# Residual rows one tile ahead, and a sum that takes its third chunk last, in a four-layer kernel

## The chip, the cores and the metric

The kernel runs on one core of a Trainium2 chip. The metric is the time of one execution on the device in microseconds (us), the median over several runs. A run has engines that work in order, each through its own queue: PE (matrix products; PEld is its weight load), DVE (vector work), ACT (activations and copies), POOL (elementwise work), and SP, which here only issues transfers (DMAs). They wait for each other through semaphores.

## The reference

Four layers on one sequence of 2048 rows by 640 columns, in float32: attention, Fourier mixing, attention, Fourier mixing, each added to its input.

```python
x = A_x
x = x + _A_ref(_layernorm(x), A_wqkv, A_wo)      # 32 heads of 20, window of 256
x = x + _B_ref(_layernorm(x), dft matrices)
x = x + _A_ref(_layernorm(x), A_wqkv, A_wo)
x = x + _B_ref(_layernorm(x), dft matrices)

def _A_ref(x, wqkv, wo):
    q, k, v = split(x @ wqkv)
    scores = where(0 <= i - j < 256, q @ k.T * 20 ** -0.5, -1e9)
    return merge(softmax(scores) @ v) @ wo
def _B_ref(x, re, im, dre, dim):
    return re @ (x @ dre.T) - im @ (x @ dim.T)
```

The change lies in the two attention layers: in `x @ wqkv` for the values (the first layer alone) and in the `x + ... @ wo` at the end (both).

## The kernel before

**Products in three parts.** Factors of the projections are split into a high and a low part, and a product of two split factors is three matmuls: high·high, high·low, low·high (`product3`, lines 253 to 260, called by `all3`). The 640 columns over which a projection sums are five chunks of 128, so a sum is 15 matmuls into one PSUM bank.

**The start of an attention layer** (`before_heads`). Rows are handled in 16 row tiles of 128. For each, `prep` requests rows, takes the mean and variance on DVE (`prep_stats`), the root on POOL (line 311), normalises on DVE (line 316), transposes on PE (line 363) and splits the transposed tile into high and low parts. The value weights come in five chunks (`value_weights`): each is loaded, copied to its high part by ACT (line 380), and its low part is the rest of a subtraction (line 383). In the first layer POOL makes the low parts of chunks 0, 1 and 2, and DVE those of 3 and 4. Chunks 0 to 2 lie in the tile `qp`, 3 and 4 in two tiles `pt`. `value(t)` then makes the two half-width sums (320 columns each, line 471) of row tile t. Row tile 0 is the first work of that kind on PE.

**The heads** (`heads`). 128 steps (8 groups of four heads by 16 row tiles) go through the engines in an order written at build time. PE makes scores twice, rows by keys (line 677) for the row maximum, which DVE takes with the mask (line 682), and keys by rows (line 705) for the exponential on ACT (line 715), which POOL masks (lines 721 and 725); line 740 multiplies by the values. The negated row maximum travels through a small transpose (line 690), a copy to the tile `mt` on ACT (line 693), and two DMAs into a row of `qp` (line 695), from where the products of line 705 take it up. Row sums travel through the DMA `sm<-ou` (line 759) to a reciprocal on DVE (line 762).

**What fills the gaps between steps** (`fill`, `more`). First comes the projection of the remaining queries and keys (`project`). When that is done, `partials` follows, in the last third of a layer's heads: for each of 16 row tiles it multiplies three of the five chunks of the heads' results by `wo` (line 275, 36 half-height matmuls), and DVE adds the sum to the row tile's residual rows. For row tiles 0 to 4 ACT first copies the sum out of PSUM (line 1046) and DVE adds it a few slots later (line 1047); from row tile 5 on DVE adds straight from PSUM (line 1050). In the profile the residual rows are the tile `big`, in `y_part(t)`, and they come by the DMAs of line 1016 (`load_y`). Row tiles 7 and 15 need three requests (112, 15 and 1 rows), since rows are stored shifted by one there.

**When residual rows are requested.** `prepare(4)`, called when the projection's last product has been written, posts the requests of the first `AHEAD_X` row tiles, row tile t after 4t slots (a step has two slots). At the head of row tile t `partials` requests row tile `t + AHEAD_X`:

```python
        elif n == 4:
            self.take_big(2, F32)
            for t in range(AHEAD_X):
                self.post(4 * t, lambda t=t: self.load_y([t]))
...
        for t in range(NB):
            sb, i = t // 4, t % 4
            self.load_y([t + AHEAD_X])
```

**The queue of transfers.** All DMAs are issued by SP, in the order of the program. They take eight semaphores in turn, and a DMA waits until the one issued eight places before it on the same semaphore has landed. So a request can start long after the place in PE's order at which the program wrote it. An instruction that reads a loaded tile waits for that DMA's semaphore, and whatever stands behind it in its engine's queue waits too.

Of the kernel before, what the change touches and what calls it, by code (L numbers as in the profile page):

```python
# [19 lines left out]
KC = D // P  # L20
# [10 lines left out]
LEAD = 10  # L31
AHEAD = 8
EARLY = 3
AHEAD_X = 2
ROWS_AT = 96
LAST_DUE = (-8, -3, 0, 4)
FIRST = 7
# [36 lines left out]
class Net:  # L74
# [336 lines left out]
    def before_heads(self, xsrc):  # L411
        nc, a = self.nc, self.a
        self.proj = self.project()
        first = self.first
        vst = [t.rearrange("p (q t c) -> p q t c", t=2, c=96) for t in self.pt[:2]]
        for v in self.pt[:2]:
            (nc.vector if first else nc.gpsimd).memset(v, 1.0)
        for t in range(6):
            self.prep_load(xsrc, t)
            if first and 2 < t < 5:  # L420
                self.load_chunk(t - 3)
        if first:
            mask = self.raw()[:, :384]
            nc.sync.dma_start(mask, a["mask"])
        self.prep_stats(0)
        self.prep_stats(1)
        self.prep_norm(0)
        state = [0, 6]
        here = self.ou + self.rr
        wv = self.wv  # L430

        def check():
            here.append(here.pop(0))
            self.check_step(here[0][:, :8 * WIDE])

        def prep():
            r = state[0]
            if state[1] < r + 5:
                self.prep_load(xsrc, state[1])
                state[1] += 1  # L440
            self.prep_stats(r + 2)
            self.prep_norm(r + 1)
            if r == 10 or r == 11:
                self.prep_norm(r + 2)
            if r == 11:
                self.prep_stats(14)
                self.prep_stats(15)
                self.prep_norm(14)
            if r == 12:
                self.prep_norm(15)  # L450
            self.prep_turn(r)
            state[0] += 1

        def pieces(sb):
            for c in range(2):
                if sb == 0:
                    prep()
                self.piece(c, sb, "q")
                if c or sb > 1 or not first:
                    check()  # L460
                if sb and state[0] < 4 * sb + 8:
                    prep()

        def value(t):
            v, xt = vst[t // 2 % 2], self.xnt(t // 4)
            rs = slice((t % 4) * P, (t % 4 + 1) * P)
            ps = []
            for hf in range(2):
                p = self.bank("v", 320)
                cs = slice(hf * 320, (hf + 1) * 320)  # L470
                self.all3(p, [((xt[:, 0, k, rs], xt[:, 1, k, rs]), (wv[k][0][:, cs], wv[k][1][:, cs]))
                              for k in range(KC)])
                ps.append(p)
            prep()
            for hf in range(2):
                dst = v[:, 4 * hf:4 * hf + 4, t % 2, 0:84].rearrange("p q (h c) -> p q h c", c=21)[:, :, :, 1:21]
                src = ps[hf].rearrange("p (q h c) -> p q h c", q=4, h=4)
                if hf == 0:
                    nc.scalar.activation(dst, src, AF.Copy)
                else:  # L480
                    nc.vector.tensor_copy(dst, src)  # L481
            if t % 2:
                nc.sync.dma_start(self.vd[:, :, t - 1:t + 1, :].rearrange("q p t c -> p q (t c)"),
                                  v.rearrange("p q t c -> p q (t c)"))
            if 3 < t < 14 or t < 4 and not first:
                check()
            elif t > 13:
                for _ in range(t - 13):
                    self.check_step()

        def values(sb):
            for i in range(4):
                value(4 * sb + i)

        def packed(sb):
            for f in self.pack(0, sb):
                f()

        self.split_w(4)
        prep()  # L500
        self.split_w(6)
        prep()
        self.split_w(3 * KC)
        for t in range(4):
            if t in (1, 2):
                self.cut_chunk(t - 1)
            value(t)
        if first:
            nc.gpsimd.tensor_copy(self.mask, mask)
        while state[1] < NB:  # L510
            self.prep_load(xsrc, state[1])
            state[1] += 1
        pieces(0)
        pieces(1)
        self.take_qk("kp", 0)
        self.ones_rows(0)
        packed(0)
        packed(1)
        values(1)
        pieces(2)  # L520
        self.load_chunk(2)
        packed(2)
        values(2)
        pieces(3)
        self.cut_chunk(2)
        self.load_chunk(3)
        packed(3)
        values(3)
        while self.stages:
            self.check_step()  # L530
        self.pt += [self.slot_tile(f"pt{i}", 3 * 512, F32) for i in (2, 3)]
        for name in ("kp", "qp"):
            self.take_qk(name, 1)
        self.ones_rows(1)
# [426 lines left out]
    def prepare(self, n):  # L961
# [28 lines left out]
# [4 lines that stand above are left out]
# [24 lines left out]
    def partials(self, xsrc):  # L1018
# [5 lines left out]
# [3 lines that stand above are left out]
            y = self.y_part(t)  # L1027
# [695 lines left out]
```

## Time and profile before

| | |
|---|---|
| median of 3 runs | 1360.11 us (1353.72 to 1364.23) |
| profiled execution, its own time | 1360.81 us |
| its span (first to last instruction) | 1359.0 us |
| mean granted PE clock | 0.989 |
| PE busy | 1292.3 us (95%) |
| DVE busy | 969.7 us (71%) |
| ACT, POOL busy | 765.1 us (56%), 733.7 us (54%) |
| DMA queue of SP | 259 MB, 63.5% of the 16 DMA engines' time |
| requests of line 1016, first attention layer | 20, from 424.5 to 508.7 us |
| requests of line 1016, second attention layer | 20, from 1094.5 to 1180.2 us |

A timeline row gives start and duration in us, engine, line, operation, the tile written and those read, and how many instructions stand together; the bracket is how long the engine sat idle before it and what released it. SPq is SP's queue of DMA issues: its duration is that of the issue, not of the transfer. In a row of stretches the numbers after each engine are its busy time and, in brackets, its instructions; then come the granted PE clock, the share of the DMA engines' time, and GB/s. Busy shares are means over stages with different limits, so a wait is judged in its own stage.

### The profile page before, as it was taken

Reading aid. Unit: us, or ns where it says so; the run is one execution under the profiler, and the core shown is the slowest. Engines: PE = TensorE matmul, PEld = TensorE weight load, DVE = VectorE, ACT = ScalarE, POOL = GpSimd, SP = SyncE. Lnnn points to the kernel's source line nnn. Section 1 sums busy time; section 2 is a strip of 40 time slices with the busy share of each in tenths; the row PEclk is TensorE's granted clock in tenths of the full one; section 3 lists DMA queues with packets and bytes.
Section 4 is the critical chain, followed back from the end, with each engine's and each line's share of the span. In section 5 each row is a group of like instructions: output and inputs, shape, how many; then the busy total and the mean of one; then the engine's idle time right before and its main releaser. Section 6 shows DMA issues by size and latency. Waiting matters only on the chain. (4 is left out here: it accounts for less than half of the span.)

```text
span 1359.0 us, 37437 instructions
## 1 busy us (share of the span) xinstructions
PE 1292.3 (95%) x13350; PEld 992.9 (73%) x13350; DVE 969.7 (71%) x3117; ACT 765.1 (56%) x1661; POOL 733.7 (54%) x1508
## 2 busy tenths in 40 slices
PE   6999999999998999999999999999999989989996
PEld 6899777777776777743689997777777767777344
DVE  7723788888887865765866247888888868658674
ACT  3322378777776665446323225777777755744472
POOL 4221677777877773310334237787777866723044
PEclk9999999999999999989999999999999989999999
DMA  5675566777677875436536755776777688671565
GB/s 198 215 226 167 188 200 199 206 195 214 201 223 219 209 235 154 135 94 210 194 117 201 227 164 185 198 207 196 220 201 225 202 217 209 197 217 47 178 209 198
DMA packets 174297, 261.49 MB, mean 192 GB/s; under 512 B 36306, under 2 KB 85586, under 8 KB 174100
## 3 DMA queue, kind: packets, MB, share of 16 engines
q1 hardware_dynamic: 174100, 259.00, 63.5%
q8 instruction: 108, 1.77, 0.6%
q14 instruction: 89, 0.73, 0.2%
HBM read 175.42 MB, written 82.31 MB: 190 GB/s over the span
## 5 line engine op out<-in xcount | busy, mean ns | idle before, releaser
L682 DVE CUSTOM_DVE_ANT_0 banks<-banks,mask 128x384 f32<-128x384 f32 (+2 forms) x1024 | 527.4, 557 | 118.7 <-PE banks L677 99.7
L715 ACT ACTIVATE pt<-banks 128x768 f32<-128x768 f32 (+2 forms) x512 | 394.4, 772 | 141.3 <-PE banks L705 72.4
L721 POOL TENSOR_SCALAR_AFFINE_SELECT pt<-pt 128x256 f32<-128x256 f32 x512 | 223.2, 436 | 181.8 <-ACT pt L715 158.7
L275 PE MATMUL banks<-big,wc 64*128 64x512 f32 x1920 | 272.5, 394 | 0.4 <-DVE pt L481 0.4
L705 PE MATMUL banks<-qp,kp 61*128 61x384 f32 (+2 forms) x1024 | 209.5, 379 | 19.6 <-DVE mc L682 14.0
L677 PE MATMUL banks<-kp,qp 60*128 60x384 f32 (+2 forms) x1024 | 209.7, 353 | 6.2 <-DVE mc L682 5.8
L740 PE MATMUL banks<-pt,vq 128*32 128x128 f32 x5760 | 211.9, 278 | 0.9 <-ACT pt L715 0.8
L275 PEld LDWEIGHTS banks<-big,wc 64*128 64x128 f32 x1920 | 187.7, 185 | 21.8 <-ACT x L590 1.5
L725 POOL TENSOR_SCALAR_AFFINE_SELECT pt<-pt 128x256 f32<-128x256 f32 x448 | 187.0, 417 | 0.0
L740 PEld LDWEIGHTS banks<-pt,vq 128*32 128x32 f32 x5760 | 142.6, 110 | 48.9 <-issue 35.2
L705 PEld LDWEIGHTS banks<-qp,kp 61*128 61x128 f32 x1024 | 107.9, 184 | 82.6 <-DVE mc L682 57.4
L677 PEld LDWEIGHTS banks<-kp,qp 60*128 60x128 f32 x1024 | 124.3, 186 | 33.6 <-DVE mc L682 22.1
L682 DVE DVE_READ_ACCUMULATOR2_ANT mc<- 128x1 f32 x1024 | 145.1, 142 | 0.0
L749 ACT ACTIVATE ou<-banks 128x128 f32<-128x128 f32 (+2 forms) x288 | 73.4, 267 | 61.9 <-PE banks L740 50.9
L257 PE MATMUL banks<-qp,big 128*128 128x320 f32 x576 | 98.4, 316 | 1.0 <-POOL qp L383 1.0
L229 POOL TENSOR_TENSOR c<-x,c 128x256 fp32r<-128x256 f32 x128 | 94.4, 745 | 0.0
L257 PEld LDWEIGHTS banks<-qp,big 128*128 128x128 f32 x576 | 88.3, 191 | 1.6 <-POOL qp L383 1.4
L257 PE MATMUL banks<-qp,kp 128*128 128x320 f32 x384 | 82.2, 347 | 6.8 <-ACT big L1132 4.4
L275 PE MATMUL banks<-big,big 64*128 64x320 f32 x912 | 80.2, 312 | 0.2 <-ACT mt L693 0.2
L257 PEld LDWEIGHTS banks<-qp,kp 128*128 128x128 f32 x384 | 61.0, 188 | 20.2 <-ACT big L1132 6.5
L1508 POOL TENSOR_TENSOR rr<-rr 128x171 f32<-128x171 f32 (+3 forms) x76 | 48.2, 644 | 49.0 <-DMA rr<-hr 18.5
L275 PEld LDWEIGHTS banks<-big,big 64*128 64x128 f32 x912 | 73.1, 189 | 0.4 <-ACT mt L693 0.4
(172 smaller groups left out, 1790.4 us busy)
## 6 DMA issues: line engine op xcount, KB each, us to landing
qk_d<-c SPq DMA_DIRECT2D x80, 512.0 KB
kp<-qk_d SPq DMA_DIRECT2D x384, 80.0 KB
qp<-qk_d SPq DMA_DIRECT2D x384, 80.0 KB
o_d<-ou SPq DMA_DIRECT2D x64, 256.0 KB
v_d<-pt SPq DMA_DIRECT2D x16, 768.0 KB
vq<-v_d SPq DMA_DIRECT2D x64, 192.0 KB
kp<-ki SPq DMA_DIRECT2D x44, 228.0 KB
big<-x SPq DMA_DIRECT2D x26, 320.0 KB
```

The costliest lines, as they stand in the source:

```text
L229: eng.tensor_tensor(out=lo[..., c], in0=src[..., c], in1=hi[..., c].bitcast(F32), op=OP.subtract)
L257: self.nc.tensor.matmul(p, x, y, start=n == 0, stop=n == last)
L275: self.nc.tensor.matmul(ps[a], x[r], y[r], start=half + i == 0, stop=half == 1 and i == n - 1, skip_group_check=True)
L677: nc.tensor.matmul(p, qp[quad % 2][b:b + 60, z, qb * P:(qb + 1) * P], kp[quad % 2][b:b + 60, z, k0 * P:(qb + 1) * P], start=True, stop=True)
L682: nc.vector.tensor_tensor_reduce(out=p, in0=p, in1=self.mask[:, 384 - n * P:], scale=1.0, scalar=NEG, op0=OP.add, op1=OP.max, accum_out=mc ...
L705: nc.tensor.matmul(self.banks[:, banks[e], :n * P], kp[quad % 2][b:b + 61, z, kb * P:(kb + 1) * P], qp[quad % 2][b:b + 61, z, kb * P:(kb + ...
L715: nc.scalar.activation(pt[quad, kb][:, 2 * z:2 * z + 2, :n * P], self.banks[:, b0:b1 + 1, :n * P], AF.Exp, scale=SCALE)
L721: nc.gpsimd.affine_select(out=t[:, :, 0:P], in_=t[:, :, 0:P], pattern=[[0, 2], [1, P]], compare_op=OP.is_ge, fill=0.0, base=0, channel_mul ...
L725: nc.gpsimd.affine_select(out=t[:, :, 256:384], in_=t[:, :, 256:384], pattern=[[0, 2], [-1, P]], compare_op=OP.is_gt, fill=0.0, base=0, ch ...
L740: nc.tensor.matmul(self.banks[32 * h:32 * h + 32, bank, :P], vq[:, 96 * (kb % 4) + 21 * h:96 * (kb % 4) + 21 * h + 32], t[:, h, (qb - kb) ...
L749: nc.scalar.activation(ou[:, dst], self.banks[:, bank, src], AF.Copy)
L1508: eng.tensor_tensor(out=t[:, lo:hi], in0=t[:, lo:hi], in1=base.broadcast_to([P, hi - lo, w]), op=op)
```

## The change

Two edits. The constant `AHEAD_X` goes from 2 to 1: `prepare(4)` posts one request and not two, and each `partials` tile requests the row tile after it and not the one after that. It holds in both attention layers. And in the first attention layer, row tile 0 of the values sums its chunks in the order 0, 1, 3, 4, 2; all other sums keep theirs.

```diff
-AHEAD_X = 2
+AHEAD_X = 1
...
                 self.all3(p, [((xt[:, 0, k, rs], xt[:, 1, k, rs]), (wv[k][0][:, cs], wv[k][1][:, cs]))
-                              for k in range(KC)])
+                              for k in ((0, 1, 3, 4, 2) if first and t == 0 else range(KC))])
                 ps.append(p)
```

On PE, at the start of the program, the two sums of row tile 0 stood so (`qp` holds the weights of chunks 0 to 2, three matmuls each, the two `pt` those of 3 and 4; line 363 is the transposes of row tiles 0 and 1 ahead and of row tile 2 behind):

```order
L363 MATMUL banks<-ident,big_109 128x128 x10
L257 MATMUL banks<-qp_113,big_164 128x320 x9
L257 MATMUL banks<-pt_115,big_164 128x320 x3
L257 MATMUL banks<-pt_116,big_164 128x320 x3
L257 MATMUL banks<-qp_113,big_164 128x320 x9
L257 MATMUL banks<-pt_115,big_164 128x320 x3
L257 MATMUL banks<-pt_116,big_164 128x320 x3
L363 MATMUL banks<-ident,big_109 128x128 x5
```

and stand so now:

```order
L363 MATMUL banks<-ident,big_109 128x128 x10
L257 MATMUL banks<-qp_113,big_164 128x320 x6
L257 MATMUL banks<-pt_115,big_164 128x320 x3
L257 MATMUL banks<-pt_116,big_164 128x320 x3
L257 MATMUL banks<-qp_113,big_164 128x320 x9
L257 MATMUL banks<-pt_115,big_164 128x320 x3
L257 MATMUL banks<-pt_116,big_164 128x320 x3
L257 MATMUL banks<-qp_113,big_164 128x320 x3
L363 MATMUL banks<-ident,big_109 128x128 x5
```

The three matmuls of chunk 2 moved behind those of chunks 3 and 4 in each half. Row 5 now holds chunk 2 of the first half and chunks 0 and 1 of the second.

On SP in the first attention layer, at the place where row tile 1 was requested (the DMAs around it are the row sums and reciprocals of lines 759 to 765, the reload of finished heads of lines 904 and 910, and, a little behind, the row maxima `mt` of line 695):

```order
 L760 DMA o_d<-ou_105 128x512
 L765 DMA r_d<-rc 128x16
-L1016 DMA big_6148<-x 128x640
 L904 DMA x<-o_d 128x1x512
 L910 DMA rr_106<-r_d 128x1x512
```

One request is gone there. Row tile 1 is now requested where row tile 2 was, seven issues earlier, and every later row tile where the one after it was.

On SP further on, around the request of row tile 7, which is the three of 112, 15 and 1 rows (`kp` and `qp` from `qk_d` are the next heads' factors, `vq` their values, `big_6191` is the tile of row tiles 8 to 15):

```order
 L640 DMA kp_1248<-qk_d 20x2x512 x3
+L1016 DMA big_6148<-x 128x640
+L640 DMA qp_1249<-qk_d 20x2x512 x3
+L667 DMA vq_100<-v_d 128x384
+L640 DMA qp_1249<-qk_d 20x2x512 x3
 L1016 DMA big_6148<-x 112x640
 L1016 DMA big_6148<-x 15x640
 L1016 DMA big_6148<-x 1x640
-L640 DMA qp_1249<-qk_d 20x2x512 x3
-L667 DMA vq_100<-v_d 128x384
-L640 DMA qp_1249<-qk_d 20x2x512 x3
-L1016 DMA big_6191<-x 128x640
```

The request of row tile 6 (one of 128 rows) now stands where row tile 7's three stood, and row tile 7's three where row tile 8's was, seven DMAs of other kinds later. The second attention layer has the same order. DVE, ACT and POOL keep their orders in both layers.

## The prediction

> **What bounds the kernel now.** I read the page first, then the timeline of each engine in the places that the change touches, then PE's waits.
>
> ```profile
> span 1359.0 us, 37437 instructions
> PE 1292.3 (95%) x13350; PEld 992.9 (73%) x13350; DVE 969.7 (71%) x3117; ACT 765.1 (56%) x1661; POOL 733.7 (54%) x1508
> ```
>
> PE is busy 95% of the span: a wait that PE loses is time gained, and a new wait of PE is time lost, unless a later wait takes it up. PE's waits between 36 and 424 us, where the first attention layer runs up to the place of the residual rows, say how much could be taken up:
>
> ```profile
> PE banks L705 <- DVE mc L682: 4.1, 8, 0.9
> PE banks L363 <- DVE big L250: 1.1, 1, 1.1
> ```
>
> These are the two largest (us in total, times, longest), and both releasers themselves follow PE's earlier work. So a shift at the start is carried on.
>
> **The first value tile.** The timeline of the start:
>
> ```profile
> 11.66 1.36 ACT L380 ACTIVATE pt<-kp 128x640 fp32r<-128x640 f32 x2
> 12.43 1.83 DVE L383 TENSOR_TENSOR pt<-kp,pt 128x640 fp32r<-128x640 f32 x2 [0.20 <-ACT pt L380]
> 12.47 2.22 PE L257 MATMUL banks<-qp,big 128*128 128x320 f32 x7
> 12.80 1.13 POOL L311 TENSOR_TENSOR rs<-rs,half 128x1 f32<-128x1 f32 x1
> ...
> 13.91 1.75 POOL L383 TENSOR_TENSOR qp<-kp,qp 128x640 fp32r<-128x640 f32 x1
> ...
> 15.71 0.56 PE L257 MATMUL banks<-qp,big 128*128 128x320 f32 x2 [1.03 <-POOL qp L383]
> ...
> 16.99 1.48 PE L257 MATMUL banks<-qp,big 128*128 128x320 f32 x9
> ```
>
> PE does six matmuls of chunks 0 and 1 and one of chunk 2, then waits 1.03 us for POOL, which finishes the low part of chunk 2 at 13.91 + 1.75 = 15.66, since a root (1.13 us) stood ahead of it. The low parts of chunks 3 and 4 are DVE's and done at 12.43 + 1.83 = 14.26; their high parts at 13.02. After the change PE goes from its sixth matmul straight to those of chunks 3 and 4. Seven matmuls in 2.22 us are some 0.27 apart at the start (each overlaps the next), so six more fill 14.2 to 15.8, and chunk 2 is then ready. What is saved is the same matmuls later, where nine take 1.48, or 0.15 apart: between 14.7 and 15.7 about four to five of them, 0.6 to 0.8 us. I take 0.7. It cannot be negative, since nothing is waited for that wasn't before; at most it is the whole wait with the tail of the matmul ahead, 1.4. No other instruction and no DMA moves here.
>
> **The request that goes.** The next rows are SP's issues in the first attention layer, one PE row that waits, and two stretches:
>
> ```profile
> 433.18 0.42 SPq L1016 DMA_DIRECT2D big<-x  x1
> 433.70 0.54 SPq L904 DMA_DIRECT2D x<-o_d  x1
> ...
> 435.64 1.66 SPq L695 DMA_DIRECT2D qp<-mt  x2
> ```
>
> ```profile
> 440.38 0.45 PE L705 MATMUL banks<-qp,kp 61*128 61x384 f32 x2 [2.15 <-DMA qp<-mt]
> ```
>
> ```profile
> 432.00:436.00 4.00, 4.00 (x60) 3.03 (x57) 2.41 (x8) 2.39 (x4) 2.55 (x6) 1.00 1.04 293
> 440.00:446.00 6.00, 5.62 (x63) 4.75 (x65) 2.97 (x11) 3.01 (x6) 2.84 (x6) 0.72 0.91 232
> ```
>
> The request at 433.18 is that of row tile 1, which the change moves up to 426. PE waits 2.15 us here for the row maxima `qp<-mt`, which stand behind it. With it gone, the issues behind come 433.70 − 433.18 = 0.5 us sooner, and 320 KB (328 thousand bytes) fewer lie ahead of them in DMA engines that are full (share 1.04, 293 GB/s): 1.1 us. Together 1.6 of the 2.15; the ends are 0 (the maxima wait for something else) and 2.15. In the second row the clock granted to PE is 0.72 over 6 us, 1.7 us lost after these waits. With a shorter wait some of that should go; I take half, 0.8, of 0 to 1.7. In the second attention layer PE shows no such wait behind 1108.27 (rows further down); I take 0.
>
> **The requests that come later.** The requests of row tiles 4 to 8 as SP issues them, in the order of the program before:
>
> ```profile
> 453.24 0.36 SPq L1016 DMA_DIRECT2D big<-x  x1
> ...
> 457.78 0.36 SPq L1016 DMA_DIRECT2D big<-x  x1
> ...
> 469.27 2.26 SPq L1016 DMA_DIRECT2D big<-x  x3
> ...
> 474.62 0.36 SPq L1016 DMA_DIRECT2D big<-x  x1
> ```
>
> These are row tiles 5, 6, 7 (three requests) and 8. After the change the same places hold 4, 5, 6 and 7. DVE takes them up here, tile by tile (4, 5, 6, 7):
>
> ```profile
> 458.16 0.82 DVE L1047 TENSOR_TENSOR big<-we,big 128x640 f32<-128x640 f32 x1
> ...
> 463.28 0.82 DVE L1050 TENSOR_TENSOR big<-banks,big 128x640 f32<-128x640 f32 x1 [0.19 <-PE banks L275]
> ...
> 470.34 0.82 DVE L1050 TENSOR_TENSOR big<-banks,big 128x640 f32<-128x640 f32 x1 [0.32 <-PE banks L705]
> ...
> 477.17 0.82 DVE L1050 TENSOR_TENSOR big<-banks,big 128x640 f32<-128x640 f32 x1 [0.19 <-PE banks L275]
> ```
>
> How long a request takes to land is read from SP's waits, since a DMA waits for the one eight places before it. Two places show it:
>
> ```profile
> 473.92 0.27 SPq L640 DMA_DIRECT2D qp<-qk_d  x1
> ```
>
> ```profile
> SPq L640 <- DMA big<-x: 0.4, 1, 0.4
> ```
>
> ```profile
> SPq L1016 <- DMA big<-x: 0.9, 1, 0.9
> ```
>
> The DMA at 473.92 is eight behind the first of 469.27 and waited 0.4 for it: 4.65 us from issue to landing. The request at 457.78 is eight behind that of 453.24 and waited 0.9 for it: 4.54. With 4.6: row tile 4 lands at 457.8, 0.3 before it is used. Row tile 5 lands at 462.4, or 464 if it queues longer, beside 463.28. Row tile 6 lands at 469.27 + 4.65 = 473.92, and DVE wants it at 470.34: a wait of 3.6 us, which takes in any wait of row tile 5. Row tile 7 is three issues now, so it lands near 474.62 + 4.6 + 0.9 = 480.1, against 477.17 + 3.6 = 480.8: covered by the wait before it.
>
> A shorter bound is the first load of the program, with little ahead of it:
>
> ```profile
> 1.69 1.38 SPq L331 DMA_DIRECT2D big<-x  x3
> ...
> 5.45 0.89 DVE L304 BATCH_NORM_STATS2 st<-big 128x6 f32<-128x320 f32 x2 [1.19 <-DMA big<-x]
> ```
>
> 3.76 us to its use, which leaves 2.7 of the 3.6. The place sits in a loaded queue, so I take 3.6. The Trainium skill, "DMA: Bandwidth & Descriptors", section "Anatomy of one DMA", fits 2.0 us plus bytes over 436 GB/s, measured on the other issuing path: an estimate of 2.75 us for this request and so a wait of 1.7. The trace's 3.76 to 4.65 disagrees, and decides.
>
> Behind the waiting add stand the mask operations of line 682, and PE waits for those at once:
>
> ```profile
> 471.75 0.33 PE L705 MATMUL banks<-qp,kp 61*128 61x128 f32 x2 [0.16 <-DVE mc L682]
> ```
>
> What a DVE wait for a DMA costs PE is shown once, in the second attention layer, where a reciprocal waited for its row sums, issued at 1099.20 (the releaser's name is that of the request eight places ahead on its semaphore, long landed):
>
> ```profile
> 1099.20 0.61 SPq L759 DMA_DIRECT2D sm<-ou  x1
> ```
>
> ```profile
> 1106.72 0.25 DVE L762 RECIPROCAL rc<-sm 128x16 f32<-128x16 f32 x1 [3.49 <-DMA big<-x_d]
> ```
>
> ```profile
> 1108.27 0.69 PE L677 MATMUL banks<-kp,qp 60*128 60x384 f32 x2 [3.11 <-DVE mc L682]
> 1108.89 1.51 PE L740 MATMUL banks<-pt,vq 128*32 128x128 f32 x24
> ```
>
> ```profile
> 1108.00:1114.00 6.00, 5.73 (x53) 4.73 (x53) 2.49 (x13) 1.84 (x5) 2.10 (x4) 0.50 0.87 276
> 474.00:480.00 6.00, 4.58 (x84) 3.79 (x78) 5.53 (x17) 3.07 (x7) 3.85 (x8) 1.00 0.68 184
> ```
>
> 3.49 us of DVE became 3.11 of PE, so 3.6 becomes 3.2. Then the granted clock was 0.50 for 6 us (half of it lost, 3.0 us). The stretch behind the new wait is not as full (4.58 busy of 6, so 1.4 us of slack): the loss is between 0 and 3.0, and I take 1.2. The Trainium skill, "TensorE: Matmul & The Clock Gate", section "What's actually happening", gives half rate after an idle window of about 3.4 us until a busy one of the same length; the 0.50 agrees, though this wait was 3.11. By it the loss would be an estimate of 1.7 us each, and the sum 1.0 higher.
>
> The same place in the second attention layer:
>
> ```profile
> 1140.39 1.09 SPq L1016 DMA_DIRECT2D big<-x_d  x3
> ```
>
> ```profile
> 1140.59 0.82 DVE L1050 TENSOR_TENSOR big<-banks,big 128x640 f32<-128x640 f32 x1 [0.31 <-PE banks L705]
> ```
>
> The request is 0.2 us ahead of its use. With 3.76 the wait is 3.6, with 4.65 it is 4.5; I take 3.6, as in the first layer: 3.2 for PE and 1.2 for the clock.
>
> The sum: −0.7 − 1.6 − 0.8 + (3.2 + 1.2) + (3.2 + 1.2) = +5.7 us. Against the profiled execution's own 1360.81 that is 1366.5. It lies 0.7 above the median of the runs, 1360.11, so the forecast for the median is 1365.8, said as 1366.
>
> **The rivals.** *The rows land in time.* With one load fewer outstanding SP runs ahead, and the place of 469.27 comes 3.6 us sooner. For it speaks that SP is behind there because it waits for landings; against it that the same DMAs, from 453.24 on, still stand between the two places. Then only the gains are left, −3.1: 1357. *The short transfer.* The rows land as the program's first load did, in 3.76 us: waits of 2.7 and 3.6, 2.3 and 3.2 for PE, too short for the clock to fall: −3.1 + 5.5 = +2.4, so 1362.5. Both landings in the busy stretch, 4.54 and 4.65, speak against it. The fit of the Trainium skill's page "DMA: Bandwidth & Descriptors" takes this further, to an estimate of 1.7 and 2.6 us, +0.5 and 1360.6. *Slower beyond doubt.* The queue becomes as long as it was for the row sums, 1106.72 − 1099.20 = 7.5 us. Then row tile 4 lands at 460.7, 2.6 late, and row tile 6 at 476.8, 3.9 later than its use shifted by that: 6.5 us in each layer, each with up to 3.0 of clock behind it: 2 × 9.5 − 3.1 = +15.9, so 1376. It decides from landings of about 7 us on; against it, landings here are 4.6 and the change takes a load out of the queue. *The gain of the queue fails.* PE's 2.15 us and the low clock behind them stay, because the maxima are late by themselves; with the two new waits that is −0.7 + 8.8 = +8.1, so 1368.
>
> **How the numbers follow.** The forecast 0.57, this last one 0.12, rows in time 0.15, short transfer 0.09, slower beyond doubt 0.07. One per cent of the time, 13.6 us, is about what a measurement of this kernel can tell from no change. Forecast, last rival, short transfer and rows in time all lie within it; above 1373.7 are the slow rival and little of the forecast's upper end (two waits of 4.5, 4.1 for PE, with 3.0 each of clock and no gain of the queue give 14.2 − 0.7 = +13.5). So slower by over 1% has 0.07, faster 0.01, within 0.92. The range goes from 1357, where the rows land in time, to 1372, which is the forecast with PE's waits at 4.1 (+2 × 0.9) and the clock's losses at 3.0 (+2 × 1.8).
>
> **What would show it.** In the profile after: no row of PE waiting for POOL's line 383 near 15.7, and the value sums about 0.7 us earlier. PE's wait for `qp<-mt` near 440 shrunk to about 0.5 and a clock near 1 behind it. DVE rows of line 1050 that wait 3 to 4 us for the DMA `big` at the seventh add of each attention layer, PE waits of like length for line 682 just behind, and a granted clock near 0.5 to 0.8 there. I am wrong if the seventh add doesn't wait, if its wait stays with DVE and doesn't reach PE, or if other row tiles wait as well.

## The result, and the profile after

The changed kernel took 1366.31 us (median of 20 runs, 1353.45 to 1372.0), the kernel before 1358.41 us (20 runs, 1353.72 to 1366.19). The ratio is 1.0054, with a 95% interval of 1.0036 to 1.0072: some 7 us slower (5 to 10), within the one per cent. The profiled execution's own time is 1370.66 us, 9.85 more than that of before, and 4.4 above the median of its kernel.

The page of the kernel after. PE is still busy 95% of the span, so its waits still count one to one:

```profile
span 1368.9 us, 37438 instructions
PE 1295.3 (95%) x13350; PEld 996.0 (73%) x13350; DVE 968.7 (71%) x3117; ACT 765.5 (56%) x1661; POOL 733.1 (54%) x1508
```

The start, in PE's timeline of the kernel after:

```profile
12.18 1.95 PE L257 MATMUL banks<-qp,big 128*128 128x320 f32 x6
13.92 1.80 PE L257 MATMUL banks<-pt,big 128*128 128x320 f32 x6
15.52 1.55 PE L257 MATMUL banks<-qp,big 128*128 128x320 f32 x9
```

PE goes without a wait from the chunks in `qp` to those in `pt` and back. The wait of 1.03 us for POOL is gone.

The first attention layer, first the place of the row maxima and the next wait of PE, in PE's timeline:

```profile
439.84 0.44 PE L705 MATMUL banks<-qp,kp 61*128 61x384 f32 x2 [0.75 <-DMA qp<-mt]
...
453.46 0.44 PE L677 MATMUL banks<-kp,qp 60*128 60x384 f32 x2 [1.33 <-DVE mc L682]
```

The wait of 2.15 us is down to 0.75, but 14 us later there is one of 1.33 that before did not have. Then row tiles 4 to 7 as DVE adds them, and the wait of PE behind the third of these:

```profile
459.76 0.82 DVE L1047 TENSOR_TENSOR big<-we,big 128x640 f32<-128x640 f32 x1
...
465.76 0.82 DVE L1050 TENSOR_TENSOR big<-banks,big 128x640 f32<-128x640 f32 x1 [0.87 <-PE banks L740]
...
475.81 0.82 DVE L1050 TENSOR_TENSOR big<-banks,big 128x640 f32<-128x640 f32 x1 [3.82 <-DMA big<-x]
...
484.79 0.82 DVE L1050 TENSOR_TENSOR big<-banks,big 128x640 f32<-128x640 f32 x1 [0.18 <-PE banks L275]
```

```profile
477.22 0.47 PE L705 MATMUL banks<-qp,kp 61*128 61x128 f32 x2 [3.66 <-DVE mc L682]
```

Row tile 6's add waits 3.82 us for its rows, and PE 3.66 us for the mask operations behind it. SP's issues of the rows of row tiles 5, 6 and 7 in the kernel after:

```profile
459.05 0.36 SPq L1016 DMA_DIRECT2D big<-x  x1
...
470.98 0.36 SPq L1016 DMA_DIRECT2D big<-x  x1
...
475.74 1.75 SPq L1016 DMA_DIRECT2D big<-x  x3
```

From the issue at 470.98 to the add at 475.81 are 4.8 us, as long as a landing was before (4.54, 4.65). Row tile 7's three requests have some 7 us to the add, and nothing waits. The add at 465.76 is put down to PE, whose instruction had long been done; the trace's record of that DMA's semaphore has row tile 5's rows landing at 465.67, so its 0.87 us is a wait for rows too. They landed 6.6 us after their issue at 459.05.

The second attention layer, DVE and PE:

```profile
1151.73 0.82 DVE L1050 TENSOR_TENSOR big<-banks,big 128x640 f32<-128x640 f32 x1 [4.76 <-DMA big<-x_d]
...
1160.67 0.82 DVE L1050 TENSOR_TENSOR big<-banks,big 128x640 f32<-128x640 f32 x1 [0.19 <-PE banks L275]
```

```profile
1153.14 0.48 PE L705 MATMUL banks<-qp,kp 61*128 61x128 f32 x2 [4.60 <-DVE mc L682]
```

The stretches around both waits (PE, PEld, DVE, ACT, POOL, then the granted clock):

```profile
472.00:478.00 6.00, 2.34 (x38) 1.75 (x37) 1.87 (x5) 1.76 (x5) 2.02 (x4) 0.87 0.83 189
478.00:484.00 6.00, 6.00 (x63) 5.21 (x61) 3.50 (x13) 2.00 (x5) 2.25 (x4) 0.56 0.62 167
1148.00:1154.00 6.00, 1.40 (x26) 1.13 (x20) 1.87 (x5) 1.24 (x4) 1.14 (x2) 0.86 0.83 209
1154.00:1160.00 6.00, 6.00 (x64) 5.22 (x62) 3.62 (x13) 1.97 (x5) 2.26 (x4) 0.57 0.66 180
```

PE gets 2.34 and 1.40 us of work into 6 us, and behind each wait its clock is 0.56 and 0.57. What the clock costs is read from the adds of row tiles 6 and 7: 6.83 us apart before (470.34, 477.17) and 8.98 after, in the second layer 7.03 and 8.94. So 2.2 and 1.9 us go behind the waits. In the trace's own record of the clock it is at half for 6.83 us at each place, from 476.47 to 483.30 and from 1152.31 to 1159.14.

### The profile page after: what moved, and what is told of

Same layout as the page of the kernel before. It is cut to its first block, busy times and chain, and to the rows that moved or that the text cites. A ratio compares the mean times of both kernels' runs of the same rounds, so it can differ in the third digit from the quotient of the medians.

```text
span 1368.9 us, 37438 instructions
## 1 busy us (share of the span) xinstructions
PE 1295.3 (95%) x13350; PEld 996.0 (73%) x13350; DVE 968.7 (71%) x3117; ACT 765.5 (56%) x1661; POOL 733.1 (54%) x1508
```

## The experiments

Each ratio is to the kernel before on the same chip. Beside it I use one more reading of the profiles: the start of the same ACT instruction in a version's profile minus its start in the profile of before, and how that difference changes over a stretch (one profiled execution of each version). Negative is a gain. "At 20" is the difference at 20 us; the other columns are changes over the stretch (times of before). The first layer's stretches hold the row maxima (430 to 448) and row tiles 3 to 6 (448 to 478), the second layer's the same places.

| version | ratio, 95% interval | at 20 | 430–448 | 448–478 | 1104–1122 | 1122–1150 |
|---|---|---|---|---|---|---|
| before | 1 | 0 | 0 | 0 | 0 | 0 |
| after | 1.0054, 1.0036–1.0072 | −1.0 | −3.7 | +9.6 | −4.5 | +8.0 |
| new sum alone | 0.9961, 0.9935–0.9987 | −0.3 | −0.1 | +0.3 | −4.3 | −0.2 |
| new sum alone, again | 0.9973, 0.9948–0.9998 | −0.8 | −2.6 | +0.5 | −5.0 | −0.6 |
| rows alone | 1.0065, 1.0036–1.0094 | +2.6 | −3.7 | +6.8 | −2.6 | +7.3 |
| rows alone, first layer | 1.0037, 1.0000–1.0074 | +2.0 | −4.1 | +4.3 | −0.1 | −0.5 |
| rows alone, second layer | 1.0040, 1.0010–1.0070 | +1.7 | −2.9 | −0.2 | −5.0 | +6.0 |
| after, row tile 6 earlier | 1.0008, 0.9989–1.0028 | −0.4 | −2.8 | +4.5 | −3.0 | +3.1 |
| after, two ahead from row tile 5 on | 0.9985, 0.9957–1.0012 | −0.5 | −4.2 | +3.8 | −2.9 | +0.2 |
| before, only row tile 6 late | 1.0064, 1.0035–1.0094 | +1.4 | −4.2 | +5.9 | −0.4 | −0.3 |
| after, row tile 6 later still | 1.0103, 1.0065–1.0141 | −1.0 | −4.3 | +10.9 | −5.0 | +10.3 |
| after, row tile 6's add later | 0.9997, 0.9968–1.0026 | −0.5 | | | | |
| new sum, rows three ahead | 1.0000, 0.9973–1.0026 | −1.2 | −1.4 | −0.3 | −1.3 | −0.4 |

The one left empty has ACT's instructions in another order, so that they can't be set against each other there.

**The two halves apart.** The new sum alone, as an edit of the changed kernel:

```diff
-AHEAD_X = 1
+AHEAD_X = 2
```

> The new order of the first value sum alone, requests two ahead as before. Theory: PE's wait of 1.03 us for POOL's line 383 is gone and the value sums end 0.7 to 1.0 us sooner; time 0.5 to 1 us less, ratio 0.9990 to 1.0000, not to be told from 1 here. Rival (the shift of the start moves the transfers against each other and the later cost comes from there): ratio 1.002 or more.

Measured: 1349.88 us, 0.9961 (0.9935 to 0.9987). And the rows alone, with the sum in its old order, again as an edit of the changed kernel:

```diff
-                              for k in ((0, 1, 3, 4, 2) if first and t == 0 else range(KC))])
+                              for k in range(KC)])
```

> Requests one tile ahead alone, the sum in its old order. Theory: all of the cost is here, ratio 1.004 to 1.007, DVE waits of 3.5 to 4.8 us at the seventh add (row tile 6) of both attention layers and a PE clock near 0.55 to 0.6 behind. Rival (the sum's order carries part of it): ratio under 1.003.

Measured: 1364.09 us, 1.0065 (1.0036 to 1.0094). So the sum is a gain and the rows are a loss, and both are larger than I had them. The start with the rows alone, PE's timeline:

```profile
15.73 0.90 PE L257 MATMUL banks<-qp,big 128*128 128x320 f32 x2 [1.35 <-POOL qp L383]
16.43 1.80 PE L257 MATMUL banks<-pt,big 128*128 128x320 f32 x6
18.03 2.60 PE L257 MATMUL banks<-qp,big 128*128 128x320 f32 x9
```

and with the new sum alone:

```profile
13.98 1.80 PE L257 MATMUL banks<-pt,big 128*128 128x320 f32 x6
15.58 2.19 PE L257 MATMUL banks<-qp,big 128*128 128x320 f32 x9
17.60 1.04 PE L257 MATMUL banks<-pt,big 128*128 128x320 f32 x6
```

With the rows alone, nine of PE's matmuls behind the wait take 2.60, some 0.27 apart, where nine at full pace take 1.48. In the profile of before it was at full pace straight behind the wait (nine in 1.48 from 16.99). That was the favourable case: of five executions with the old sum it is the only one, the others reach that pace between 18.8 and 21.6 us. Eight executions with the new sum reach it between 14.9 and 16.9. In all thirteen, the spacing changes where the trace's record of the granted clock begins: in the profile of before at 14.89, inside its wait, and with the rows alone at 21.56. At 20 us the old sum stands at 0, +1.4, +1.7, +2.0, +2.6 (mean 1.5) and the new one between −0.3 and −1.2 (mean −0.7): the order is worth 2.2 us, not 0.7.

**The new sum alone, once more**, the same kernel, since it is the fastest version found:

> The kernel with the new order of the first value sum alone (rows two ahead), timed in more rounds, since its gain of 0.4 per cent rests on three. Theory (the new order saves about 2.1 us at the start, 0.5 to 1 us of wait and the rest because PE doesn't fall back to its slow spacing behind that wait; the further 3 us of the first measurement are other executions' scatter): 0.9985, between 0.997 and 0.9995. Rival (the prediction's term, 0.7 us): 0.9995, not to be told from 1. Rival (the first measurement as it stands): 0.996.

Measured: 1350.46 us, 0.9973 (0.9948 to 0.9998). Together with the first measurement that is about 0.9967, 4.5 us faster than before, of which the start shows 2.2. The rest lies within the two intervals, and no stretch that this edit touches shows more.

**Row tile 6 alone earlier.** In the changed kernel row tile 6 is requested together with 5, at the head of row tile 4:

```diff
-            self.load_y([t + AHEAD_X])
+            self.load_y({4: [5, 6], 5: []}.get(t, [t + AHEAD_X]))
```

> The changed kernel, but row tile 6 is requested at the head of row tile 4 together with row tile 5; row tile 7 still one ahead. Theory (the time goes by when a row lands against its add): row tile 6 no longer waits, row tile 7, whose wait was covered, now does, 2 to 3 us in each attention layer; ratio 1.000 to 1.003. Rival (row tile 6 is the only tight place): no wait at any add, ratio 0.996 to 0.999. Second rival (the cost comes from the queue's changed order and not from the wait): ratio stays at 1.005.

Measured: 1356.2 us, 1.0008 (0.9989 to 1.0028). Row tile 6's wait is gone in both layers and with it 0.0046 of the ratio, 6.2 us. The wait of 2 to 3 us that I expected at row tile 7 in its place did not come. In the first layer 4.5 us stay, at row tile 5 and at a reciprocal, and in the second 3.1, where a reciprocal waits 2.82 us. DVE in the first layer:

```profile
465.03 0.83 DVE L1050 TENSOR_TENSOR big<-banks,big 128x640 f32<-128x640 f32 x1 [1.88 <-DMA big<-x]
...
468.91 0.25 DVE L762 RECIPROCAL rc<-sm 128x16 f32<-128x16 f32 x1 [2.01 <-DMA x<-o_d]
```

**Row tile 6 alone late.** The kernel before, with row tile 6 requested at the head of 5 and everything else as it was:

```diff
-            self.load_y([t + AHEAD_X])
+            self.load_y({4: [], 5: [6, 7]}.get(t, [t + AHEAD_X]))
```

> The kernel before, with one thing late: row tile 6 is requested one tile later, just ahead of the three requests of row tile 7, in both attention layers. All else is two ahead. Theory: this alone makes the wait, 3 to 5 us of DVE at the seventh add, 3 to 4.6 of PE, a clock near 0.6 behind; ratio 1.005 to 1.008 (nothing gained elsewhere). Rival (the cost comes from all requests being later): ratio under 1.003.

Measured: 1361.9 us, 1.0064 (1.0035 to 1.0094). This one late request costs as much as all of them together. The first layer shows it as in the changed kernel, DVE and then PE:

```profile
477.06 0.82 DVE L1050 TENSOR_TENSOR big<-banks,big 128x640 f32<-128x640 f32 x1 [4.74 <-DMA big<-x]
```

```profile
478.47 0.47 PE L705 MATMUL banks<-qp,kp 61*128 61x128 f32 x2 [4.58 <-DVE mc L682]
```

The second layer hardly does. SP's issue of row tiles 6 and 7, and DVE's add:

```profile
1139.09 2.77 SPq L1016 DMA_DIRECT2D big<-x_d  x4
```

```profile
1143.94 0.82 DVE L1050 TENSOR_TENSOR big<-banks,big 128x640 f32<-128x640 f32 x1 [0.98 <-DMA big<-x_d]
```

The landing takes the same 4.8 us, but SP reached the request 3.9 us before DVE wanted the rows (1143.94 − 0.98 = 1142.96); in the changed kernel it was 0.6 us behind (1147.57 against 1151.73 − 4.76 = 1146.97). So the wait is the landing less SP's lead, and the lead differs from one execution to the next. How often the second layer waits in this version, and so how the 0.0064 (some 8.7 us) divide between the layers, is open: its one profile shows 5.9 us in the first and nothing in the second.

**Row tile 6 later still**, requested at its own head in the changed kernel:

```diff
-            self.load_y([t + AHEAD_X])
+            self.load_y({5: [], 6: [6, 7]}.get(t, [t + AHEAD_X]))
```

> The changed kernel, with row tile 6 requested one more tile later, at its own head (seven DMAs further on, some 5 us). Theory (wait and time go one for one): DVE waits 8 to 10 us at the seventh add in each attention layer, ratio 1.012 to 1.016. Rival (a longer wait is taken up by work that PE has ahead, or the clock's loss is already spent): ratio under 1.010.

Measured: 1368.91 us, 1.0103 (1.0065 to 1.0141; six runs). DVE and PE in the first layer:

```profile
473.21 0.82 DVE L1050 TENSOR_TENSOR big<-banks,big 128x640 f32<-128x640 f32 x1 [8.17 <-DMA big<-x]
```

```profile
474.62 0.47 PE L705 MATMUL banks<-qp,kp 61*128 61x128 f32 x2 [8.02 <-DVE mc L682]
```

DVE's wait less 0.15 us is PE's, here (8.17, 8.02) as in the changed kernel (3.82, 3.66; 4.76, 4.60) and above (4.74, 4.58). The loss behind it, from the distance of the next add (8.27 us against 6.83), is 1.4 us, no more than behind a wait half as long: the clock is at half from 468.84 to 479.08, but more than half of that passes while PE still waits. The second layer waits alike (DVE 8.96, PE 8.81). So the wait grows as forecast, and the time by less than the 1.012 to 1.016 of the theory.

**From row tile 5 on two ahead again**, in the changed kernel, so after a start with one ahead:

```diff
-            self.load_y([t + AHEAD_X])
+            self.load_y([t + 1] if t < 3 else [4, 5] if t == 3 else [t + 2])
```

> The changed kernel, but from row tile 3 on requests are two ahead again: row tiles 4 and 5 at the head of row tile 3, 6 at 4, 7 at 5 as before; only the request of row tile 1 beside that of row tile 0 and the order of row tiles 2 and 3 stay changed. Theory: no add waits, the shorter wait for the row maxima in the first attention layer and the 0.7 to 1 us of the start are kept: ratio 0.997 to 0.999, 1 to 4 us less than before. Rival (the gain of the removed request is taken back by the next full stretch of the queue): ratio 0.9990 to 1.001.

Measured: 1353.64 us, 0.9985 (0.9957 to 1.0012). No add waits for rows in either layer. In the first one 3.8 us of the 4.2 gained at the row maxima are still lost, now at a reciprocal that waits for its row sums (the two loads at one place lie ahead of these in the queue, which I take for the cause but didn't test apart):

```profile
469.09 0.25 DVE L762 RECIPROCAL rc<-sm 128x16 f32<-128x16 f32 x1 [2.53 <-DMA sm<-ou]
```

**One attention layer at a time**, as an edit of the kernel before, so with the old sum; for the first layer alone (and with 1 and 2 exchanged for the second alone):

```diff
-            for t in range(AHEAD_X):
+            for t in range(1 if self.first else 2):
...
-            self.load_y([t + AHEAD_X])
+            self.load_y([t + (1 if self.first else 2)])
```

> Requests one ahead in the first attention layer only, old order of the sum. Theory by the sum of the prediction: two gains of 1.6 and 0.8 us against a wait of 3.2 to 3.7 and a clock loss of 1.2 to 2.6: +2 to +4 us, ratio 1.0015 to 1.003. Rival (the gain at the row maxima is lost again a few steps further): ratio 1.003 to 1.005.

Measured: 1357.49 us, 1.0037 (1.0000 to 1.0074). DVE's adds of row tiles 5 and 6:

```profile
461.60 0.82 DVE L1050 TENSOR_TENSOR big<-banks,big 128x640 f32<-128x640 f32 x1 [1.47 <-DMA big<-x]
...
471.44 0.82 DVE L1050 TENSOR_TENSOR big<-banks,big 128x640 f32<-128x640 f32 x1 [2.78 <-DMA big<-x]
```

> Requests one ahead in the second attention layer only, old order of the sum. Theory: no gain, a wait of 3.2 to 4.6 us and a clock loss of 1.2 to 2.6: +4.4 to +7 us, ratio 1.003 to 1.005. Rival (both layers alike): the same ratio as for the first layer alone.

Measured: 1360.15 us, 1.0040 (1.0010 to 1.0070); row tile 6's add waits 4.66 us and PE 4.50, and the first layer, which is as before, shows neither. The two layers make 1.0077 together, beside 1.0065 for both at once: each pays for itself, about half. The one profile of the first layer alone doesn't show its loss (−4.1 and +4.3 in the two stretches of that layer).

**The add later.** In the changed kernel the requests stay, but row tiles 5 and 6 are also copied by ACT and added two slots later:

```diff
-            if self.step < 16 * (NQ - 1) - 4:
+            if t < 7:
```

> The changed kernel, but row tiles 5 and 6 of the partial results are also copied out of PSUM by ACT and added two slots later (two slots are half a step's pair, some 2 to 3.5 us here), as row tiles 0 to 4 are; the requests stay one row tile ahead. Theory (the seventh add waits because its rows land about 3.8 and 4.8 us after its place in DVE's order, and everything behind it waits with it): the add's place moves back by two slots, so its wait falls from 3.82 and 4.76 us to 0.5 to 2, PE's wait behind it likewise, and about half to all of the 11 us of the two layers comes back: 1.000 to 1.002 of the kernel before, 3 to 6 us faster than the changed kernel's 1.0054. Rival (PE's wait is for the PSUM bank or the row maxima, and the add is only where it shows): no change, 1.005. Second rival (ACT's two further copies delay the exponentials behind them): a wait of PE for ACT of about 0.6 us per copy, which leaves 1.002 to 1.004.

Measured: 1354.67 us, 0.9997 (0.9968 to 1.0026). Row tile 6's adds on DVE, first and second layer:

```profile
475.99 0.83 DVE L1047 TENSOR_TENSOR big<-we,big 128x640 f32<-128x640 f32 x1 [1.59 <-DMA big<-x]
```

```profile
1139.79 0.83 DVE L1047 TENSOR_TENSOR big<-we,big 128x640 f32<-128x640 f32 x1 [2.65 <-DMA big<-x_d]
```

The waits fall by 2.2 and 2.1 us, to 1.59 and 2.65, and the ratio by 0.0057, 7.7 us. That is more than the waits alone, and the clock behind them is at half for less time: not at all in the first layer and for 3.41 us in the second. Much of what the late rows cost hangs on the add's place in DVE's order: what stands behind it waits with it.

**More lead.** The new sum with the rows three ahead:

```diff
-AHEAD_X = 1
+AHEAD_X = 3
```

> The changed kernel with the rows requested three row tiles ahead, and the new order of the first value sum. Theory (two ahead is already enough, no add of the kernel before waits for rows, so a further tile of lead has nothing to save): no row of lines 1047 or 1050 that waits for rows, and the time of two ahead with the new sum order, 0.996 of the kernel before (0.994 to 0.999). Rival (one more load early in the layer's last third delays the small transfers of row maxima and row sums behind it): PE's wait for the row maxima near 440 grows from 2.1 to 3 or 4 us and the whole is 0.998 to 1.001.

Measured: 1354.65 us, 1.0000 (0.9973 to 1.0026). It brings nothing over two ahead (0.9973 on the same chip). I expected 0.996 and no add that waits for rows; PE's wait for the row maxima, which the rival had growing to 3 or 4 us, is 1.74 us (at 436.17). But one add waits for rows in each layer, that of row tile 2 (DVE):

```profile
441.62 0.82 DVE L1047 TENSOR_TENSOR big<-we,big 128x640 f32<-128x640 f32 x1 [1.81 <-DMA big<-x]
```

```profile
1106.42 0.95 DVE L1047 TENSOR_TENSOR big<-we,big 128x640 f32<-128x640 f32 x1 [3.07 <-DMA big<-x_d]
```

For row tile 2 the edit doesn't do what it says. With two ahead it is requested at the head of row tile 0; with three, `prepare(4)` posts it after eight slots, and SP gets to it at 436.02, 13.8 us after the issue that now holds row tile 3 (422.25).

## Why the prediction was right, and where its steps were not

The forecast, 1366 us and within one per cent, held (1366.31). Its mechanism carried the result; several of its terms were wrong in size, and they partly made up for each other. That the time is met to 0.3 us is luck: the kernel before took 1358.41 us over 20 runs, 1.7 less than over the three that the forecast was set on, and the change cost 7.9 us between the medians (7.3 by the ratio), for 5.7.

*The first value sum.* Taken at −0.7. Against the one profile of before that is what eight executions show (mean −0.7). Against the kernel before as it mostly runs it is −2.2. The step that failed is "behind the wait the matmuls are 0.15 apart": in four of five executions of the old order they are 0.27 apart for 3.1 to 5.8 us more. The bound of 1.4 was too low for the same reason.

*The request that goes.* The wait at 440 was to shrink by 1.6 of 2.15; it went to 0.75, by 1.4, and the clock of 0.72 behind it went to 1.00. That is the edit and not chance: five of six profiled executions with the request in place wait 1.7 to 2.15 us for `qp<-mt` there, for instance the new sum alone,

```profile
440.34 0.69 PE L705 MATMUL banks<-qp,kp 61*128 61x384 f32 x2 [2.10 <-DMA qp<-mt]
```

and one none; seven without it wait 0 to 0.81. The whole gain of 3.7 us between 430 and 448 is not the edit's: the six with the request lie between 0 and −4.2 (mean −1.9), six without it between −2.8 and −4.3 (mean −3.8). The difference of the means, 1.9, stands beside the 2.4 of the sum, but the scatter of one group is as large. The rival in which this gain fails has its condition against it, since the wait and the low clock did go; its +8.1 us lies no further from the measured 7.3 to 7.9 than the forecast's 5.7, so the time alone would not have told the two apart.

In the second layer the term was 0. There the wait of the reciprocal, whose 3.49 us served as the price of a wait, is shorter in all six versions with one ahead that can be compared (2.5 us or less, the stretch −2.6 to −5.0), but the stretch is also shorter in two of six with more (−4.3, −5.0). A gain of about 2 us is possible there; the runs do not settle it.

*Row tile 6 late.* The mechanism is as forecast, at the forecast add and in both layers, and the versions that move this request alone (earlier, late, later still), with the one that moves the adds of row tiles 5 and 6, show it to be the cause. The sizes: DVE waits of 3.82 and 4.76 for 3.6 and 3.6, PE 3.66 and 4.60 for 3.2 and 3.2. The step "3.49 became 3.11" was a poor price; behind row tile 6's add PE takes over all but 0.15 us each time. For the second layer I had 3.6 to 4.5 and took the lower end. Behind the waits I took 1.2 us of clock; it was 2.2 and 1.9, with a granted clock of 0.56 and 0.57. The estimate of 1.7 that the Trainium skill's page "TensorE: Matmul & The Clock Gate", section "What's actually happening", gave is nearer, though the record has the clock at half for 6.83 us, twice what that estimate took. Over the versions, behind DVE waits of 2.2 us and more at row tile 6, the next add comes 1.0 to 2.2 us late, but not with the first layer alone, where the clock stays full behind 2.78 us. The short transfer, with waits of 2.7 and 3.6, is out; from issue to add are 4.8 and 4.2 us, not 3.76. That rival also called waits of 2.3 and 3.2 us too short for the clock to fall. The profile of before spoke against it (0.72 behind 2.15 us), and with the rows alone the clock fell to half behind PE's wait of 2.03.

*What I had at nothing.* In the first layer 448 to 478 costs 9.6 us in the profile of after, and the step at row tile 6 only 3.7 + 2.2 = 5.9 of them. The other 3.7 come before it: the PE wait of 1.33 at 453.46 (a reciprocal ahead of it waited 1.32 us for its row sums), a clock of 0.72 over 454 to 460, and row tile 5's 0.87. The 1.33 us are this execution's own: none of the other profiles has a wait of line 677 of 0.7 us or more there. With the clock behind them they make up most of the 3.7, and nothing shows them to be the edit's. Row tile 5's wait comes from the edit, and all five versions with it one ahead in this layer and its add in place have one (0.87 to 2.72 us). The prediction said row tile 5 is about even and any wait of its own is taken from row tile 6's. The term behind it that was too small is the landing: 4.6 us, or some 6 if it queues, where row tile 5's rows took 6.6 us here, 5.8 with the first layer alone and 7.9 with the rows alone. In part its wait is taken from row tile 6's: with the rows alone the two waits are 2.72 and 2.18, with the first layer alone 1.47 and 2.78, here 0.87 and 3.82, so 4.3 to 4.9 together, for 3.6. "Other row tiles wait as well" was one of the ways in which I said I would be wrong, and here I was. Row tile 7 is covered, as forecast.

*The sum.* Of the 9.85 us between the two profiled executions the places of the edits hold −1.0 − 3.7 + 9.6 − 4.5 + 8.0 = +8.4; the other 1.5 lie where nothing was changed. Against the forecast of −0.7 for the start, +2.0 for the first layer and +4.4 for the second, that is −1.0, +5.9 and +3.5. By the ratio it is +7.3 (4.9 to 9.8), for +5.7. So the loss is larger than I had it in the first layer, and the start gives more back than one profile showed. The rows alone times the mean of the new sum, 1.0065 × 0.9967 = 1.0032, lies just under the interval of the change itself and well within what the two factors' own intervals allow. The intervals here are 0.2 to 0.4 per cent to either side, so the one per cent that the prediction took as the least that can be told from no change was too wide.

## What to carry to other kernels

Price a later request as its landing time (at the waiting adds of row tiles 5 and 6 between 3.7 and 7.9 us) less the lead with which the issuing queue reaches it, and charge the whole wait to whoever stands behind the waiting instruction, with a second charge for the clock; a deferred add, or one request moved, takes most of it back without any change of the rest. Before a stall in one profile is entered as the gain or the price of an edit, see whether it is there in a second execution: stretches that no edit touched differed here by 4 to 6 us.

## What the runs showed of the hardware

**A short wait near the start costs more than itself.** Behind 1.03 to 1.35 us of idle PE, the matmuls stayed at 0.27 us apart for 3.1 to 5.8 us in four of five executions, and in one not at all; that one and one of the four waited the same 1.03 us. The granted clock in the profile's rows is 1.00 in these stretches, but only because the trace's record of it has no entry there: it begins where the spacing becomes 0.15, at 14.89 us in the profile of before and between 18.79 and 21.56 in the four. The Trainium skill, "TensorE: Matmul & The Clock Gate", section "What's actually happening", says that full rate comes after a busy window of about 3.4 us of a window that runs freely, and that the count of slow matmuls differs from run to run; the spacing and its scatter agree with that.

**The granted clock does not follow the length of one wait alone.** Over the stretches from 478 to 484 and from 1154 to 1160 it was 0.56 to 0.58 behind PE's 3.66, 4.58 and 4.60. Behind shorter waits it went either way: 0.72 over 454 to 460 behind 1.33 in the changed kernel, 1.00 behind 2.62 with the first layer alone. The trace's record of the clock shows what the length leaves out. In all thirteen executions the clock is either full or half, and it changes only at whole multiples of 3.413 us after the record's first entry. As far as the rows tell, what counts is how much PE does in one such piece. With the first layer alone, the wait of 2.62 us (470.23 to 472.85) is parted by the edge at 471.16, and PE is busy for 2.48 and 1.73 us of the two pieces:

```profile
467.75:471.16 3.41, 2.48 (x46) 1.89 (x42) 0.91 (x4) 2.06 (x6) 2.20 (x4) 1.00 0.82 235
471.16:474.58 3.42, 1.73 (x24) 1.73 (x26) 3.01 (x9) 0.46 (x2) 0.86 (x2) 1.00 0.83 176
474.58:477.99 3.41, 3.09 (x56) 2.64 (x54) 2.96 (x10) 1.99 (x4) 1.87 (x5) 1.00 0.55 170
```

With the rows alone, a shorter wait of 2.03 us (473.19 to 475.22) lies within one piece, PE is busy for 1.39 us of it, and the next piece is at half:

```profile
472.12:475.54 3.42, 1.39 (x30) 1.00 (x31) 1.73 (x5) 1.47 (x4) 1.53 (x3) 1.00 0.80 207
475.54:478.95 3.41, 3.41 (x31) 3.06 (x31) 1.92 (x8) 0.77 (x2) 1.16 (x3) 0.50 0.73 180
```

Over the thirteen executions, all 26 pieces at full clock in which PE was busy for less than 0.44 of the time were followed by one at half, and 8 of 35 between 0.44 and 0.63. That is not the whole rule: nine pieces near 600 and 1271 us, in which the rows show PE always busy, were followed by half as well, which stays open.

**A DVE operation held up by POOL.** In 5 of 13 profiled executions, 4.9 to 6.1 us are lost near 307 us, where the program is the same in all of them. One subtraction of line 229 on DVE took 4.8 us in these five. Here in the second measurement of the new sum alone, and then in the kernel before:

```profile
301.90 4.82 DVE L229 TENSOR_TENSOR wc<-x,wc 128x384 fp32r<-128x384 f32 x1
```

```profile
302.91 0.62 DVE L229 TENSOR_TENSOR wc<-x,wc 128x384 fp32r<-128x384 f32 x1
```

PE waits behind it, again in the second measurement of the new sum alone:

```profile
307.05 0.47 PE L677 MATMUL banks<-kp,qp 60*128 60x128 f32 x2 [3.54 <-DVE mc L682]
```

POOL worked through that time without a gap, each instruction at its usual length (same execution, first and last):

```profile
302.15 0.42 POOL L721 TENSOR_SCALAR_AFFINE_SELECT pt<-pt 128x256 f32<-128x256 f32 x1
...
305.57 0.74 POOL L229 TENSOR_TENSOR c<-x,c 128x256 fp32r<-128x256 f32 x1
```

In the kernel before, POOL's instruction beside the subtraction was the longer one, 0.75 for 0.42:

```profile
303.05 0.75 POOL L721 TENSOR_SCALAR_AFFINE_SELECT pt<-pt 128x256 f32<-128x256 f32 x1
```

So one of the two gave way, and where it was DVE, it got on only when POOL's run ended (306.3). The Trainium skill, "GPSIMD Engine Reference", section "Specifications", says that the two share their interfaces to SBUF and that DVE operations with two SBUF inputs contend with POOL; this one has two. The rows agree; that this is the cause was not tested. A step of that size in some executions is a third to a half of the 10 to 20 us between the fastest and the slowest run of one kernel; how often it comes in the runs that were not profiled is not known.
